# Keys and values by halves of a chunk: narrower scores and outputs in a fused attention and MLP kernel

## The chip, the cores and the metric

The kernel runs on one core of a Trainium2 chip. A core has TensorE (PE in the profile, the matrix engine; PEld is its loading of weights), VectorE (DVE), ScalarE (ACT), GpSimd (POOL) and SyncE (SP, which here only issues DMAs), and 16 DMA engines that SP, ACT and POOL share through queues of their own. The metric is device time in microseconds of one launch. The median of three runs before is 204.6 us (204.56 to 204.68).

## The reference

Two stages follow each other. The first is a linear attention with decay over 4 batches, 8 heads, 768 positions and 64 features, in blocks of 64 positions:

```
Dmask = where(rel >= 0, lam ** rel, 0)            # rel = query position - key position, in a block
intra = (q_block @ k_block.T * Dmask) @ v_block
inter = (q_block * lam ** (pos + 1)) @ kv_state
out   = intra + inter
kv_state = lam ** 64 * kv_state + (k_block * lam ** (63 - pos)).T @ v_block
```

The block size does not change what is computed: a query sees every key at or before its own position, with the weight lam to the power of the distance. The second stage is an MLP over the 3072 rows (4 x 768) of 512 features that come out: `silu(x @ w_in) @ w_out` with 2048 features in between. Inputs and output are float32.

## The kernel before

**The attention.** The kernel works with chunks of 128 positions, and with pairs of chunks: pair n (0 to 11) holds 256 positions of one batch, for all 8 heads. `load_pair` (L426) issues one DMA each for k, q and v of a pair on SP. Partition p of the tile holds positions 2p and 2p + 1 of the pair, for each head, so a row of the transfer is two positions of 64 float32 numbers, 512 bytes. The first chunk is in partitions 0 to 63, the second in 64 to 127 (`halves`), and r = 0 or 1 is the parity of the position.

`prepare` (L526) casts k and q to bfloat16 in `kq` (`cast`, or `cross` from pair 4 on, which swaps heads in the second chunk), scales v by a power of lam in `vd` (`scale_v`, with the constants `lam_v`), and turns kq into `kqT`: by TensorE for pairs 0 to 3 (L578), by a DMA transpose on SP from pair 4 on (L593).

From pair 3 on the matmuls of the attention stand in a `burst` (L603). A burst holds, for the new pair n, the sums of k times v for the state (`state`, L659, named d) and the scores (`score`, L670, named s); and, for the pair before, the outputs from the masked scores (`output`, L626, named o) and from the state (`inter64`, L633, named i). All these matmuls are 64 rows by 64 columns, a quarter of the array, and two lists, `rows[0]` and `rows[1]`, feed the two halves of the array's rows, so that four run at once. A score matmul takes 64 keys of one parity as weights and streams all 128 queries of the chunk, 64 of each parity. An output matmul takes v of 64 keys of one parity as weights and streams the masked scores of these keys, 128 columns. A burst is cut into up to three parts: up to the last output, up to the last score of heads 0 to 3 (k below 2), and the rest. All its banks (two for outputs, one for the state, four for scores) are taken when its first part is placed.

After a part with scores, VectorE multiplies each bank of them with the 0/1 constant `tri` (`mask`, L825, 128x512) into `st`. VectorE evacuates outputs with the powers of lam into `xt`, the input of the MLP (`evac`, L719).

**The MLP.** `product1` (L921) computes x @ w_in, ScalarE applies silu while it empties the banks (L951), and `product2` (L972) computes the second product. For the last 12 units of 128 rows the second product is made by seven products of quarter matrices in place of eight (`product2_of_four`, L1063), for the last 8 units the first product too (`product1_of_four`, L1214). They need sums of quarters of the weights: `sums_of_w_out` (L1035) builds five sums `bsum` of w_out, each in two halves on VectorE or POOL. The same function has a second way, for the sums listed in `BMOVED`: a copy by a DMA on SP and an accumulating DMA issued by POOL. BMOVED is empty here.

**What sets the order.** Everything is a task with a key, a cost per engine, the tasks it depends on and the buffers it needs. `Planner` (L57) replays all tasks by these costs, takes at each engine the ready task with the lowest key, and so writes out one fixed order for each engine and each DMA queue. Two tables correct it by hand or by search: `SHIFT` moves keys, `HOME` pins a task to an engine. Where PE is planned to be idle in the first 19 us, filler matmuls on `ones` are put (L1321).

Of the kernel before, what the change touches and what calls it, by code (L numbers as in the profile page):

```python
# [36 lines left out]
WIDE, CAST, LARGE, PLAIN, TURN = (512, 24.0, 27.0), (256, 14.0, 31.0), (2048, 92.0, 92.0), (2048, 84.0, 84.0), (1024, 46.0, 46.0)  # L37

# [18 lines left out]
class Planner:  # L57
# [8 lines left out]
    SHIFT = {('cast', 10, 1, 0): -0.5, ('cast', 10, 1, 1): -2.5, ('cast', 6): -3.5, ('cast', 7, 1, 0): -1.5, ('first', 2): -0.5,  # L66
             ('first', 2, 6): -8, ('first', 3, 6): -8.5, ('first', 4, 4): 1, ('first', 5, 0): -4, ('first', 5, 6): -0.5,
             ('first', 6): 6.25, ('first', 6, 11): 2.25, ('first', 6, 12): -1, ('first', 6, 14): 13.25, ('first', 6, 15): 2.25,
             ('first', 6, 2): 0.5, ('first', 6, 3): 0.25, ('first', 6, 4): -4.5, ('first', 6, 5): -10.75, ('first', 7): -0.25,
             ('first', 7, 0, 4): 1.75, ('first', 7, 1, 4): 1, ('first', 7, 2, 3): 1, ('first', 8, 0, 5): -4,  # L70
             ('first', 8, 1, 1): -3.5, ('first', 8, 2, 4): 4.5, ('four', 12): 4.5, ('four', 20): -0.75, ('group', 2): 0.25,
             ('group', 3): -5.5, ('group', 7): 4.75, ('group', 8): -7.5, ('load w', 3, 1): -1.5, ('mask', 11): 5.75, ('mask', 5): 3,
             ('mask', 7, 0, 1): 3, ('mask', 8, 0, 0): 5.75, ('mask', 9, 0, 1): 0.25, ('outputs', 0, 0): 4, ('pair', 10): 2.5,
             ('pair', 11): -9.75, ('pair', 4): -7.5, ('pair', 5): -0.75, ('pair', 9): 8.75, ('scale', 3, 0): -1, ('score', 1): 8,
             ('second', 10): 7, ('seven', 12): 0.5, ('seven', 12, 3): -8.25, ('seven', 12, 5): -4.75, ('seven', 16): 3.75,
             ('seven', 20): 3.75, ('silu', 8, 1, 0, 1): 2.75, ('states', 2, 0): 6.75, ('store', 9): -2, ('turn', 3, 0, 1): -10.75,
             ('turned', 1): -7.25, ('u3', 8): 5.5, ('w', 1): 6.75, ('xe', 0, 0, 1): 4.5, ('xe', 11): 11.75, ('xe', 3, 0, 0): 1.5,
             ('xf', 6): -10.25, ('xt', 7, 1): 7, ('y', 10, 0, 0): 5.75}
    HOME = {('a', 16, 1, 1): 'POOL', ('a', 20, 5, 0): 'POOL', ('a', 20, 5, 1): 'POOL', ('b', 3, 1): 'POOL',
            ('cast', 11, 1, 1): 'POOL', ('cast', 3, 0, 1): 'ACT', ('cast', 4, 0, 0): 'DVE', ('cast', 5, 0, 0): 'POOL',  # L80
            ('cast', 5, 1, 0): 'POOL', ('cast', 5, 1, 1): 'ACT', ('cast', 6, 0, 0): 'DVE', ('cast', 6, 1, 0): 'DVE',
            ('cast', 6, 1, 1): 'ACT', ('cast', 7, 1, 0): 'DVE', ('cast', 7, 1, 1): 'ACT', ('cast', 8, 1, 1): 'DVE',
            ('cast', 9, 0, 0): 'POOL', ('cast', 9, 1, 0): 'POOL', ('cast o', 1, 1): 'DVE', ('cast o', 2, 0): 'ACT',
            ('cast o', 2, 1): 'ACT', ('cast w', 1, 3): 'POOL', ('m3', 12): 'DVE', ('result', 1): 'ACT', ('scale', 11, 0): 'POOL',
            ('scale', 9, 0): 'POOL', ('to u', 7, 3): 'DVE', ('turned', 0, 0, 1): 'DVE', ('turned', 0, 1, 0): 'ACT',
            ('u3', 8, 0): 'DVE', ('u3', 8, 1): 'ACT', ('u3', 8, 2): 'ACT', ('w', 3, 0): 'POOL', ('w', 4, 0): 'POOL',
            ('x', 7, 3): 'POOL', ('x', 8, 1): 'POOL', ('xe', 6, 0, 0): 'POOL', ('xe', 6, 0, 1): 'POOL', ('xe', 7, 0, 0): 'ACT',
            ('xf', 10, 0, 1): 'POOL', ('xf', 4, 0, 1): 'DVE', ('xf', 7, 0, 0): 'POOL'}
# [197 lines left out]
def kernel(  # L286
# [10 lines left out]
    nc = tc.nc  # L297
# [12 lines left out]
    AWAY, XAWAY, OWN = range(5,12), (), (0, 1)  # L310
# [5 lines left out]
    BMOVED, POOLED = (), (6,)  # L316
    LOADED, MOVED, HEAD = (4, 9), (12,16), (1.8, 1.8, 1.2, 0.6)
    TKEY, SEVENS, LAG, WSKEY, FIRST_SEVENS = 9.0, 12, 5.0, 14.0, (16,20)
# [77 lines left out]
    lam_be = const.tile([128, NP], F32, name="lam_be")  # L396
    for r in range(2):
        nc.scalar.activation(lam_v[:, :, r], log_all, AF.Exp, scale=pose[:, r:r + 1])
# [27 lines left out]
    def load_pair(key, n, which):  # L426
# [4 lines left out]
        def plain(e, i, g, ms):  # L431
            nc.sync.dma_start(out=tile_of(bufs[i, g], [128, 2 * len(ms), 128], F32, "raw"),
                              in_=src[i][heads(ms)].rearrange("h (p r) d -> p h (r d)", r=2))

        for g, ms in enumerate(parts_of(n)):
            for i in which:
                bufs[i, g] = Buf("rawh" if n in FINE else "raw")
                ts[i, g] = add((key, g, i), {"SP": 0.55}, lambda e, i=i, g=g, ms=ms: plain(e, i, g, ms), bufs=[bufs[i, g]],
                               nbytes=0.131 * len(ms), kind=WIDE,
# [43 lines left out]
    def rates(e):  # L483
        for a in range(NP):
            nc.scalar.activation(lam_xe[:, a, :], row, AF.Exp, scale=log_lam[:, a:a + 1])

# [116 lines left out]
    def burst(n, alone=False):  # L603
# [72 lines left out]
        def queue(row, what, width, fn, *more, part=slice(None)):  # L676
            rows[row].extend([(what, 0.0005 + 0.00044 * width, lambda a=(k, r) + more: fn(*a), k) for k, r in steps][part])
# [708 lines left out]
```

## Time and profile before

| What | Value |
|---|---|
| Median of three runs | 204.6 us (204.56 to 204.68) |
| Profiled execution: its time, its span | 204.5 us, 202.8 us |
| VectorE, ScalarE, POOL busy | 146.2, 123.4, 71.4 us |
| HBM read, written | 27.27 MB, 6.29 MB |
| Packets on SP's DMA queue (q1) | 62400, 34.74 MB, 62.4% of 16 engines' span |
| On ACT's queue (q10), on POOL's (q0) | 7.2%, 14.4% |
| PE matmuls: score L670, output L626, state L659 | 288, 288, 240 |

The span runs from the first to the last instruction; the time has 1.7 us more around it. Busy time of PE counts a matmul from its start to its modelled end, and neighbours overlap. The share of a DMA queue is the sum of its packets' times over 16 engines and the span. A wait is put down to the instruction that ended it.

### The profile page before, as it was taken

How to read it: one execution, taken by the hardware profiler on the slowest of the kernel's cores; microseconds unless marked ns; L12 is line 12 of the kernel's file. 1: busy time of each engine (PE TensorE's matmuls, PEld its weight loads, DVE VectorE, ACT ScalarE, POOL GpSimd, SP SyncE). 2: the span in 40 equal slices, each digit the busy share in tenths (PEclk: the TensorE clock that was granted, in tenths of full speed). 3: DMA queues.
4: the chain of work that ended last, by engine and by line, in shares of the span. 5: the costliest groups of instructions: out<-in, count | busy, mean ns of one | idle time of the engine just before them, and what ended most of it. 6: DMA issues, size and time to landing. Idle time of an engine off the chain costs nothing.

```text
span 202.8 us, 6082 instructions
## 1 busy us (share of the span) xinstructions
PE 196.8 (97%) x2585; PEld 145.3 (72%) x2585; DVE 146.2 (72%) x231; ACT 123.4 (61%) x193; POOL 71.4 (35%) x84
## 2 busy tenths in 40 slices
PE   6999999999999999999999999999999999999993
PEld 2776887867865557557776465458888888888882
DVE  3697749778994949599795875969765766743972
ACT  3697887849785655705384626683796878564010
POOL 4105430222560400058766041338954372000800
PEclk9999999999999999999999999999999999999999
DMA  4999999999999999899999471119997967111324
GB/s 110 339 335 366 386 362 334 368 313 382 230 282 261 318 344 298 208 311 218 303 255 213 130 128 33 57 58 222 176 184 184 218 179 136 52 55 52 107 103 155
DMA packets 71658, 44.43 MB, mean 219 GB/s; under 512 B 18448, under 2 KB 64528, under 8 KB 71632
## 3 DMA queue, kind: packets, MB, share of 16 engines
q1 hardware_dynamic: 62400, 34.74, 62.4%
q0 software_dynamic: 5456, 4.46, 14.4%
q10 hardware_dynamic: 3776, 4.86, 7.2%
q8 instruction: 20, 0.33, 0.6%
q14 instruction: 6, 0.05, 0.1%
HBM read 27.27 MB, written 6.29 MB: 165 GB/s over the span
## 4 chain that ended last, share of the span: by engine, by line
PE 90%; DVE 5%; issue 2%; ACT 1%; ACTq 0%
PE banks L935 27%; PE banks L1126 18%; PE banks L977 17%; PE banks L1254 12%; PE banks L1321 4%; PE banks L626 2%; PE banks L670 2%; PE banks L578 2%; DVE kq L409 1%; DVE xt L414 1%; PE banks L633 1%; DVE st L414 1%; PE banks L659 1%; PE banks L848 1%; PE banks L898 1%
## 5 line engine op out<-in xcount | busy, mean ns | idle before, releaser
L935 PE MATMUL banks<-xt,w_in_bf 128*128 128x256 bf16 (+1 forms) x448 | 67.4, 288 | 0.4 <-DVE xt L414 0.2
L951 ACT ACTIVATE g<-banks 128x512 bf16<-128x512 f32 x64 | 46.0, 745 | 26.8 <-PE banks L935 25.4
L935 PEld LDWEIGHTS <-w_in_bf 128*128 128x128 bf16 x448 | 42.9, 98 | 15.3 <-issue 0.8
L977 PE MATMUL banks<-w_out_bf,g 128*128 128x512 bf16 x192 | 49.6, 379 | 0.0
L414 DVE TENSOR_TENSOR st<-banks,tri 128x512 bf16<-128x512 f32 (+1 forms) x42 | 29.9, 757 | 3.7 <-PE banks L670 2.9
L977 PEld LDWEIGHTS <-g 128*128 128x128 bf16 x192 | 18.3, 98 | 19.1
L414 DVE TENSOR_TENSOR xt<-banks,lam_xe 128x512 bf16<-128x512 f32 x24 | 16.0, 684 | 12.5 <-PE banks L626 12.3
L1126 PE MATMUL banks<-bsum,g 128*128 128x256 bf16 x160 | 21.2, 273 | 0.0
L407 ACT ACTIVATE kq<-raw 64x512 bf16<-64x512 f32 (+3 forms) x24 | 18.5, 799 | 2.7 <-DMA raw<-in_k_dram 1.2
L407 ACT ACTIVATE osb<-banks 128x512 f32<-128x512 f32 (+1 forms) x15 | 8.7, 582 | 17.5 <-PE banks L977 12.2
L1126 PEld LDWEIGHTS <-asum 128*128 128x128 bf16 x176 | 17.2, 98 | 2.0
L409 DVE CAST kq<-raw 64x512 bf16<-64x512 f32 (+3 forms) x21 | 15.2, 741 | 4.0 <-DMA raw<-in_k_dram 2.5
L1126 PEld LDWEIGHTS <-g 128*128 128x128 bf16 x160 | 15.6, 98 | 1.9
L414 POOL TENSOR_TENSOR xf<-y,lam_be 128x256 f32<-128x256 f32 (+1 forms) x11 | 8.2, 749 | 22.1 <-DVE y L789 21.9
L1017 DVE TENSOR_TENSOR asum<-g 128x1024 bf16<-128x1024 bf16 x11 | 9.1, 836 | 8.3 <-PE banks L1126 2.9
L1270 ACT ACTIVATE g<-tmp 128x512 bf16<-128x512 f32 x16 | 12.4, 774 | 3.5 <-DVE tmp L1017 3.3
L1017 DVE TENSOR_TENSOR tmp<-banks,tmp 128x512 f32<-128x512 f32 x16 | 11.0, 687 | 4.8 <-PE banks L1254 4.1
L414 DVE TENSOR_TENSOR vd<-raw,lam_v 128x1024 bf16<-128x1024 f32 (+1 forms) x11 | 12.3, 1120 | 3.0 <-DMA raw<-in_v_dram 2.9
L1254 PE MATMUL banks<-xsum,wsum 128*128 128x256 bf16 x96 | 14.4, 273 | 0.0
L1017 POOL TENSOR_TENSOR asum<-g 128x1024 bf16<-128x1024 bf16 x3 | 6.4, 2121 | 22.8 <-PE banks L1126 19.1
L1254 PEld LDWEIGHTS <-wsum 128*128 128x128 bf16 x128 | 12.4, 98 | 1.5
L1321 PE MATMUL banks<-ones 128*128 128x128 bf16 (+1 forms) x85 | 11.0, 277 | 1.9 <-DVE ones L358 1.5
(96 smaller groups left out, 294.6 us busy)
## 6 DMA issues: line engine op xcount, KB each, us to landing
raw<-in_k_dram SPq DMA_DIRECT2D x11, 512.0 KB, 5.4
raw<-in_q_dram SPq DMA_DIRECT2D x11, 512.0 KB, 6.1
raw<-in_v_dram SPq DMA_DIRECT2D x11, 512.0 KB, 7.6
out_dram<-osb ACTq DMA_DIRECT2D x18, 256.0 KB, 3.6
raw_w<-in_moe_w_in_dram SPq DMA_DIRECT2D x8, 512.0 KB, 8.0
raw_w<-in_moe_w_out_dram SPq DMA_DIRECT2D x8, 512.0 KB, 6.6
asum<-g SPq DMA_DIRECT2D x8, 256.0 KB, 2.6
asum<-g POOLq DMA_DIRECT2D x8, 256.0 KB, 5.1
```

The source lines that it names most:

```text
L407: nc.scalar.activation(o, i, AF.Copy)
L409: nc.vector.tensor_copy(o, i)
L414: (nc.vector if e == "DVE" else nc.gpsimd).tensor_tensor(o, a, b, op=AL.mult)
L578: nc.tensor.transpose(t[:, r, m, :], kq_of()[:, i, r, 2 * m:2 * m + 2, :], ident)
L935: nc.tensor.matmul(t[:, j, :], lhsT=w_in_bf[:, ko, 128 * m:128 * m + 128], rhs=xt[gi].tile[:, ko, :], start=(ko == 0), stop=(ko == KI - 1))
L951: nc.scalar.activation(t.rearrange("p j (c a r) -> p (j c) r a", c=n // U, r=2), psum_of(bank).rearrange("p (jc r a) -> p jc r a", r=2, a= ...
L977: nc.tensor.matmul(psum_of(bank), lhsT=gs[gi, ko][1](1, 128 * gp, 128)[:, 0], rhs=w_out_bf[:, ko], start=(ko == 0), stop=(ko == KO - 1))
L1017: (nc.vector if e == "DVE" else nc.gpsimd).tensor_tensor(o, x, y, op=op)
L1126: nc.tensor.matmul(part(bank, u), lhsT=lhs(u), rhs=b_of(ko), stop=ko == 7, skip_group_check=True, start=opens and not ko and not u)
L1254: nc.tensor.matmul(two_of(bank)[:, f], lhsT=(wb[0].tile if wb else w_quarter(*wl))[:, ko, fs], rhs=(xsum(xr) if isinstance(xr, int) else x ...
L1270: nc.scalar.activation(t.rearrange("p j (c a r) -> p (j c) r a", c=2, r=2), src().rearrange("p (jc r a) -> p jc r a", r=2, a=64), AF.Silu)
L1321: nc.tensor.matmul((t if b.pool == "bank" else t[:, 0])[:, 0:w], lhsT=ones[:, 0:128], rhs=ones[:, 0:w], start=True, stop=True)
```

## The change

In pairs 4 to 11 (`SPLIT`) k and v are laid out by halves of a chunk in place of parities: a partition holds, for each chunk, one position of its first half and one of its second. q keeps its layout. Rows of the k and v transfers are one position, 256 bytes, and each transfer is three DMAs: one of 128 partitions for the two middle quarters of the pair, and two of 64 partitions for the first and the last quarter. In the first chunk the early half is at r = 0, in the second at r = 1, so the code takes `r ^ i` or `r ^ c` where it means early (0) or late (1).

No query of a chunk's first half can see a late key. So the scores of late keys are made for late queries alone (64 columns in place of 128), in a layout of their own: banks of group 0 hold the early keys of all heads, banks of group 1 the late keys, and the masked scores `st` and the outputs follow this. The masks of group 1 are 128x256. New constants `lam_s` and `tri_s` serve the new order of positions. The two banks of group 1 are taken only when the part of the burst that first writes them is placed. The order inside a burst has the early keys of all heads ahead of the late ones.

BMOVED becomes (1, 7, 6), so three of the five sums of w_out are made by DMAs. The tables SHIFT and HOME are replaced as a whole, so the planner's order differs from beginning to end: pairs 5, 7 to 11 stand later among the matmuls, pairs 4 and 6 a little earlier.

```diff
+HALF = (256, 16.5, 16.5)
...
-    SHIFT = {...}
-    HOME = {...}
+    SHIFT = {...}
+    HOME = {...}
...
+    SPLIT = range(4, 12)
...
-    BMOVED, POOLED = (), (6,)
+    BMOVED, POOLED = (1, 7, 6), (6,)
...
         def plain(e, i, g, ms):
+            if n in SPLIT and i != 1:
+
+                t = tile_of(bufs[i, g], [128, 2 * len(ms), 128], F32, "raw")
+                x = src[i][heads(ms)].rearrange("h (s a) d -> a s h d", a=64)
+                nc.sync.dma_start(out=t[:, :, 64:128], in_=src[i][heads(ms), 64:192].rearrange("h p d -> p h d"))
+                for c, p in enumerate(halves):
+                    nc.sync.dma_start(out=t[p, :, 0:64], in_=x[:, 3 * c])
+                return
             nc.sync.dma_start(out=tile_of(bufs[i, g], [128, 2 * len(ms), 128], F32, "raw"),
                               in_=src[i][heads(ms)].rearrange("h (p r) d -> p h (r d)", r=2))
...
+    def split_rates(e):
+        for r in range(2):
+            nc.scalar.activation(lam_s[:, :, r], log_all, AF.Exp, scale=pose_s[:, r:r + 1])
+
+    def split_masks(e):
+        for c, r in enumerate(halves):
+            nc.gpsimd.iota(spot_s[r], pattern=[[64 - 128 * c, 2]], base=64 * c, channel_multiplier=1)
+        nc.gpsimd.tensor_scalar(pose_s, spot_s, -1.0, 64.0, op0=AL.mult, op1=AL.add)
+        nc.gpsimd.memset(tri_s, 1.0)
+        for r in halves:
+            nc.gpsimd.affine_select(
+                out=tri_s[r], in_=tri_s[r], compare_op=AL.is_ge, fill=0.0,
+                base=0, pattern=[[1, 2], [2, 64]], channel_multiplier=-1,
+            )
...
-                 lam_v[:, hs, :, None].to_broadcast([128, n_h, 2, 64]))
+                 (lam_s if n in SPLIT else lam_v)[:, hs, :, None].to_broadcast([128, n_h, 2, 64]))
...
                 for h, d in enumerate(halves):
-                    nc.tensor.matmul(psum_of(ob[c])[d, U * k:U * k + U], lhsT=o["vd"].tile[halves[c], 2 * k + h, r, :],
-                                     rhs=o["st"][k // 2].tile[halves[c], 2 * h + k % 2, U * r:U * r + U],
+                    to = psum_of(ob[c])[d, U * k:U * k + U]
+                    if o["n"] not in SPLIT:
+                        by = o["st"][k // 2].tile[halves[c], 2 * h + k % 2, U * r:U * r + U]
+                    else:
+                        by = o["st"][r].tile[halves[c], 4 * h + k]
+                        if r:
+                            to = to.rearrange("d (q i) -> d q i", q=2)[:, :, 32:]
+                    nc.tensor.matmul(to, lhsT=o["vd"].tile[halves[c], 2 * k + h, r ^ c if o["n"] in SPLIT else r, :], rhs=by,
                                      start=first_in(boxes[c], h), stop=True, skip_group_check=True)
...
-            db, sb_ = Buf("bank", n % NB != NB - 1), [[Buf("bank", True) for _ in halves] for _ in range(2)]
+            db, sb_ = Buf("bank", n % NB != NB - 1), [[Buf("bank", not g or n not in SPLIT) for _ in halves] for g in range(2)]
...
-            bufs += [db, kq, vd, kqT] + sum(sb_, [])
+            bufs += [db, kq, vd, kqT] + (sb_[0] if n in SPLIT else sum(sb_, []))
+            late_bufs = sb_[1] if n in SPLIT else []
...
                     h = row ^ i if n in CROSSED else row
+                    if n in SPLIT:
+
+                        t = psum_of(sb_[r][h])[:, 0:4 * U // (1 + r)].rearrange("p (m q i) -> p m q i", m=4, q=2)
+                        nc.tensor.matmul(t[c, k], lhsT=t_of()[halves[row], 0, r ^ i, k, c],
+                                         rhs=t_of()[halves[row], 1, :, k, c.start + 32 * r:c.stop], start=k == 0, stop=True,
+                                         skip_group_check=True)
+                        continue
...
+                if new and late_bufs and any(what == "s" and k for what, k, _, _ in order[prev:cut]):
+                    bufs, late_bufs = bufs + late_bufs, []
...
+                        if n in SPLIT:
+                            t = tile_of(st, [128, 8, U // (1 + g)], BF16, "st")[:, 4 * h:4 * h + 4]
+                            mult(e, t.rearrange("p m (q i) -> p m q i", q=2),
+                                 psum_of(b)[:, 0:4 * U // (1 + g)].rearrange("p (m q i) -> p m q i", m=4, q=2),
+                                 tri_s[:, :, 0:64 // (1 + g)][:, None].to_broadcast([128, 4, 2, 64 // (1 + g)]))
+                            return
...
+    masks_s = add((-4.9, 0), {"POOL": 1.2}, split_masks, tag="masks s")
...
+    rates_s = add((-3.2, 0), {"ACT": 0.4}, split_rates, deps=[masks_s], tag="rates s")
```

## The prediction

> **What bounds the kernel now.** I read the page from the top: busy shares, slices, chain.
>
> ```profile
> span 202.8 us, 6082 instructions
> PE 196.8 (97%) x2585; PEld 145.3 (72%) x2585; DVE 146.2 (72%) x231; ACT 123.4 (61%) x193; POOL 71.4 (35%) x84
> ...
> PEclk9999999999999999999999999999999999999999
> DMA  4999999999999999899999471119997967111324
> ...
> PE 90%; DVE 5%; issue 2%; ACT 1%; ACTq 0%
> ```
>
> TensorE (PE) is busy 97% of the span at the full granted clock and is 90% of the chain that ended last. A busy PE need not be a PE at its peak, so I asked next what PE waited for; this is the whole answer.
>
> ```profile
> PE banks L1321 <- DVE ones L358: 1.5, 1, 1.5
> PE banks L1321 <- DVE st L414: 0.3, 1, 0.3
> PE banks L935 <- DVE xt L414: 0.2, 1, 0.2
> PE banks L898 <- PE banks L879: 0.2, 1, 0.2
> PE banks L626 <- PE banks L633: 0.2, 1, 0.2
> ```
>
> Behind the first 31 us there is hardly a wait. The end is set by the length of PE's instruction stream, and PE time saved there is a gain of the same size, as long as nothing new makes PE wait. The other resource at its limit is the DMA; these rows of the table by stretches give span, PE, PEld, DVE, ACT, POOL, clock, DMA share (over 1 where queues overlap) and GB/s.
>
> ```profile
> 31.00:62.00 31.00, 31.00 (x384) 23.15 (x377) 25.91 (x38) 24.29 (x38) 9.87 (x10) 1.00 1.08 319
> 62.00:112.00 50.00, 49.67 (x733) 31.80 (x731) 38.84 (x60) 25.80 (x40) 19.68 (x21) 1.00 1.12 269
> 112.00:143.00 31.00, 31.00 (x461) 18.68 (x459) 24.31 (x42) 18.01 (x28) 11.82 (x14) 1.00 0.50 108
> ```
>
> Until 112 us the 16 DMA engines are full, then half idle. PE does not notice, since its order takes every pair well behind the pair's arrival. So two sums are wanted: PE's work, and how much later the loads may come.
>
> **Scores and outputs (L670, L626).** The change makes the matmuls of late keys 64 columns wide in place of 128, in pairs 4 to 11. Their matmuls use a quarter of the array each, four at a time. The price of a width is in the timeline of before, where some of L761 are 64 wide and L898 and L626 are 128 wide (start, duration, ..., count):
>
> ```profile
> 10.02 0.32 PE L761 MATMUL banks<-vd,kq 64*64 64x64 bf16 x16
> 15.99 0.44 PE L761 MATMUL banks<-vd,kq 64*64 64x64 bf16 x32
> 20.23 0.42 PE L898 MATMUL banks<-st,vd 64*64 64x128 bf16 x16
> 108.05 0.64 PE L626 MATMUL banks<-st,vd 64*64 64x128 bf16 x32
> ```
>
> 16 more matmuls are four quartets: (0.44 - 0.32)/4 = 30 ns for a quartet 64 wide, (0.64 - 0.42)/4 = 55 ns for one 128 wide. A pair has 32 score and 32 output matmuls, that is 8 quartets of each, and half of them become short: 8 x 25 ns = 0.2 us a pair, 1.6 us over eight pairs. All of it lies on the path. Both ends of this price: nothing, if the strided 2x32 writes into the bank cost what the narrower stream saves (no row shows such a write); 8 x 8 x 27.5 = 1.8 us if a short one takes exactly half. I take 1.6, since both rows are of this array form.
>
> **Banks taken later.** Only the last part of a burst now asks for the two banks of the second half. In the order of the changed kernel's instructions PE has 29 visits to quartet work where it had 27 (pair 3's burst and pair 7's are cut in two, with other matmuls between). A visit costs filling and draining: the visit of before from 107.54 to 109.14 in the chain is 1.60 us with 112 matmuls (28 quartets; the 24 state matmuls beside scores cost less than full ones, so the two rows of the array add up to 0.22 + 1.14 = 1.36), which leaves 0.24. Two more: 0.5 us lost. Two more filler matmuls (L1321) are 0.1.
>
> **Masks (L414 on st).** The 16 masks of late keys shrink from 128x512 to 128x256: 757 ns by their group against 359 to 399 ns for other 128x256 VectorE results, so about 0.36 x 16 = 5.8 us less on VectorE. Three sums of w_out (six of the ten bsum instructions, L1017: 1081 ns on VectorE, 2549 on POOL) become DMAs, of which VectorE is spared five: 5.4 us more. VectorE is 72% busy and not on the path, so I count nothing for it directly, but the only late stall of PE, between 90.5 and 92.0 (about 0.65 us longer than the matmuls need), is for xt behind two slow casts on VectorE. The whole order is laid out anew, so that place is gone and another may appear: between 0 and 0.65 us of gain I take 0.3.
>
> **New constants.** Six small POOL instructions (two iota, one tensor_scalar, one memset, two selects; their like in before took 0.31 + 0.28 + 0.31 + 0.89 = 1.8 us) go where POOL is idle from 3.2 to 9.5 us. Two Exp on ScalarE (0.49 us for the two of L398) go into its idle 0.84 us ahead of the first kqT copy at 6.44. Cost nothing; without that cover 0.5 us, since the kqT copy leads to the first scores.
>
> **Loads.** A load of k or v becomes three DMAs: 16 loads, 32 more issues on SP at 0.45 to 0.57 us, some 16 us of SP, which is not the limit: one pair is 7 issues (3.5 us) and one transpose (2.7 to 4.8 us) per 10 us of transfers. The row size falls from 512 to 256 bytes, 1024 packets to 2048. In the packet records of before, SP's queue took (medians) 27 ns for 512 bytes, 46 for 1024 and 84 for 2048: 8 ns and 37 ns per KB, so 17.5 ns for 256. The 16,384 packets of 256 bytes there (the transposes of kq) have a median of 18 and a mean of 28. Bounds: 17.5 and 28. I take 18, because loads lie on the straight line of the loads and a transpose is another kind of transfer. Then a split load takes 2048 x 18/16 = 2.3 us for 1.75, and 16 of them add 9 us to a full queue.
>
> Does PE feel it? Adding transfers in SP's order (512 KB loads 1.75, weights 1.34, transposes 3.6 us from 2.8 us on) puts the end of the transposes of pairs 4 to 10 in before at 57.6, 68.2, 77.0, 87.7, 94.8, 103.6 and 112; the trace has their packets at 52-57, 60-68, 72-76, 84-88, 88-96, 100-104 and 112-116, so the sum holds within some 2 us. For the changed order the same sum gives 57.5, 73.8, 79.1, 91.4, 103.6, 111.3, 119.0 and 128.4 for pairs 4 to 11. PE's bursts move too: counting the matmuls ahead of each (109 ns for 256 columns, 216 ns for 512), they stand 0.3 earlier, 4.8 later, 2.0 earlier, then 3.1, 3.1, 2.6, 0.9 and 4.9 later, so near 62.2, 78.8, 85.0, 99.6, 110.3, 118.8, 125.8 and 140.1. With 1 us to land, the margins are 3.7, 4.0, 4.9, 7.2, 5.7, 6.5, 5.8 and 10.7 us, where late pairs had over 11 before. Hidden, but with half of the cover gone. Pair 10 has 15 split loads ahead of its transpose, so 5.8 us are used up at 5.8/15 = 0.39 us more per load: 3 ns more per packet, 21 ns. That is the point from which the loads decide.
>
> The three sums by DMA (three copies on SP, three accumulates on POOL, 512 KB each) come behind the last v load, when the share has fallen to 0.5. The asum copies queue behind them on SP; in before they wait for activations until 134.7, so 2 x 1.75 us ahead costs nothing. The transpose of pair 11 shares the engines with two accumulates: 1024 packets of 65 ns (POOL's queue) are 4.2 us each, within its 10.7.
>
> [...]
>
> **Sum.** -1.6 (columns) + 0.5 (visits) + 0.1 (fillers) - 0.3 (stall) = -1.3 us. The profiled execution took 204.5 us (span 202.8 and 1.7 around it), 0.1 under the median of 204.6. So 203.2 on the profiled one, 203.3 for the median.
>
> **The rivals.**
> 1. The gain is eaten (no change, 204.2 to 205.0): the visits stay, the head of 31 us, where PE follows VectorE and ScalarE, loses 0.5 to 1 us by its new order. For it: the first 31 us have the PE waits of before. Against: POOL and ScalarE have gaps there that the new instructions fit. About 204.6.
> 2. The loads come late (slower): 256-byte packets cost over 21 ns. At 28 ns, (28 - 21) x 2048/16 x 15 = 13.4 us: 217. At 24.5 ns half of that: 210. For it: the full DMA until 112 us and the mean of 28. Against: the line through three sizes and the median of 18.
> 3. The late banks make PE wait (slower). The last part of eight bursts asks for two banks while the matmuls behind it on PE, of any kind, stand in line; if a bank still waits for its eviction (745 ns for a silu, 684 for xt) PE stands for half of one, 0.35 us, each time: 8 x 0.35 = 2.8 us against 1.3, so 206.1. It decides from 1.3/8 = 0.16 us a burst. For it: four score banks were all taken ahead of the burst before, so this wait could not occur there. Against: PE's idle time after 31 us was 0.65 us in all, so evictions as a rule come in time.
>
> **How the numbers follow.** Forecast 0.58 (own range 202.4 to 204.0), no change 0.12, late loads 0.12, late banks or other waits of that size 0.18. A median of this kernel can be told from another from about 0.2% (0.4 us). Faster is the first, same the second, slower the sum of the last two, 0.30. Low: 1.8 + 0.65 us gained and one visit fewer gives 202.3. High: late banks at 0.4 us each give 206.6; beyond it lie most of the late loads (0.10), some of the late banks (0.04) and 0.06 lie under the low end.
>
> **What would show it.** Right: PE's share stays at 97% or above, short score and output quartets at 30 ns, PE's waits after 31 us under 1 us in sum, 256-byte load packets at 18 ns, the DMA row full until about 120 us. Wrong: PE waiting for kq, vd or kqT (late loads), PE's quartets waiting inside a burst for ACT or DVE on banks (late banks), 256-byte packets over 21 ns, or short quartets at 55 ns.

## The result and the profile after

The changed kernel takes 223.22 us (median of 6 runs, 222.31 to 225.27) against 204.58 us for the kernel before (6 runs, 204.49 to 204.68): a ratio of 1.092, interval 1.087 to 1.097. It is 18.6 us slower, where 1.3 us of gain was forecast, and far outside the range. The profiled execution took 225.27 us, 2.05 over the median. Ratios leave out executions that took over 1.5% more than the fastest of the same kernel (two of eight in e4, two of ten in f3, two of four in g4, one each in e7 and h2), so some differ a little from the quotient of the medians beside them, which take in all. In the changed kernel the same operations have other line numbers: L991 and L1033 are the plain matmuls of the two products, L1310 and L1182 those of the groups of units that are made by seven products of quarter matrices (Winograd groups below), L708 the scores in the layout by halves, L662 the outputs, L1382 the fillers.

The head of the page, after:

```profile
span 223.6 us, 6126 instructions
PE 199.9 (89%) x2574; PEld 145.4 (65%) x2587; DVE 139.1 (62%) x234; ACT 121.4 (54%) x190; POOL 69.7 (31%) x89
...
PEclk9999999999999999999999999999969967999999
DMA  4999999999999999999799999999999789702244
...
PE 44%; DMA 30%; SPq 14%; DVE 4%; POOL 3%; issue 2%; ACT 1%; POOLq 0%; DVEq 0%
```

TensorE falls from 97 to 89% of the span, and the chain that ended last is now 30% DMA and 14% SP's queue, neither of which was in it before. The DMA row is full until about 173 us, where it had been half idle from 112 to 143. The granted clock drops in three slices late in the span. The answer on what PE waited for (us in total, times, longest) gives the places:

```profile
PE banks L1182 <- DMA asum<-g: 8.2, 2, 5.6
PE banks L708 <- DMA kqT<-kq: 4.4, 2, 3.5
PE banks L1382 <- DVE ones L359: 1.5, 1, 1.5
PE banks L1033 <- POOL w_out_bf L417: 1.1, 1, 1.1
PE banks L991 <- POOL w_in_bf L417: 1.0, 1, 1.0
```

g is the output of silu, which the second product reads. For two of its three Winograd groups (units 12 to 19) the sums of quarters of g, `asum`, are made by the DMA: copies on SP and accumulating DMAs issued by POOL. The first line is the wait for these sums, the second is late loads of k and q (kqT is the transposed pair). Both had no line before. Around the first wait the table by stretches (columns as in the prediction) shows the other loss:

```profile
160.00:180.00 20.00, 14.13 (x114) 11.41 (x112) 9.37 (x14) 9.22 (x15) 8.47 (x10) 0.91 1.03 160
180.00:200.00 20.00, 17.28 (x138) 14.63 (x139) 7.36 (x12) 10.64 (x17) 7.57 (x7) 0.83 0.74 132
```

PE is not only idle there but slow, at a granted clock of 0.91 and 0.83, and the busy time itself is longer: its matmuls of 256 columns take 213 ns from start to start where this trace has the clock at a half, 109 elsewhere. The two waits are 12.6 us, and the lower clock over these 40 us is worth by estimate up to 1.8 + 3.4 us more (20 x 0.09 and 20 x 0.17).

The packet records of the trace say what became of the transfers. On SP's queue the mean of a 512-byte packet is 28.0 ns before and 32.2 after; of the 256-byte packets of the loads by halves the median is 18 to 19 ns, about the forecast, but the mean is 22 to 23 in the stretches of 8 us that hold no transpose (40 to 48 and 64 to 72 us). What makes the reading turn is when this begins: already in the first 40 us, where no load by halves exists and the loads are those of before, 512-byte packets have a mean of 30.5 to 32.7 ns in stretches of 8 us, for 27.0 to 28.2 before. Something makes packets longer that the diff does not touch.

### The profile page after: what moved, and what is told of

It reads as the page before. It is cut to its first block, busy times and chain, and to the rows that moved or that the text cites. A ratio compares the mean times of both kernels' runs of the same rounds, so it can differ in the third digit from the quotient of the medians.

```text
span 223.6 us, 6126 instructions
## 1 busy us (share of the span) xinstructions
PE 199.9 (89%) x2574; PEld 145.4 (65%) x2587; DVE 139.1 (62%) x234; ACT 121.4 (54%) x190; POOL 69.7 (31%) x89
## 4 chain that ended last, share of the span: by engine, by line
PE 44%; DMA 30%; SPq 14%; DVE 4%; POOL 3%; issue 2%; ACT 1%; POOLq 0%; DVEq 0%
PE banks L1182 14%; PE banks L991 12%; PE banks L1033 11%; DMA asum<-g 10%; DMA raw_w<-in_moe_w_out_dram 6%; DMA bsum<-w_out_bf 5%; SPq L622 5%; PE banks L1310 4%; SPq L446 4%; DMA raw_w<-in_moe_w_in_dram 3%; DMA kqT<-kq 3%; DMA raw<-in_q_dram 2%; SPq L1106 2%; SPq L444 2%; DVE st L420 2%
## 5 line engine op out<-in xcount | busy, mean ns | idle before, releaser
L991 PE MATMUL banks<-xt,w_in_bf 128*128 128x256 bf16 (+1 forms) x447 | 60.9, 288 | 1.1 <-POOL w_in_bf L417 1.0
L1007 ACT ACTIVATE g<-banks 128x512 bf16<-128x512 f32 x64 | 45.6, 742 | 15.9 <-PE banks L991 11.7
L991 PEld LDWEIGHTS <-w_in_bf 128*128 128x128 bf16 x448 | 42.8, 98 | 15.4 <-issue 1.2
L1033 PE MATMUL banks<-w_out_bf,g 128*128 128x512 bf16 x180 | 42.7, 379 | 2.2 <-POOL w_out_bf L417 1.1
L1033 PEld LDWEIGHTS <-g 128*128 128x128 bf16 x192 | 18.0, 98 | 19.4 <-issue 0.2
L413 ACT ACTIVATE kq<-raw 64x512 bf16<-64x512 f32 (+2 forms) x24 | 18.5, 799 | 21.0 <-DMA raw<-in_q_dram 12.3
L1182 PEld LDWEIGHTS <-asum 128*128 128x128 bf16 x176 | 18.1, 104 | 11.7 <-DMA asum<-g 8.8
L1182 PE MATMUL banks<-bsum,g 128*128 128x256 bf16 x160 | 23.0, 275 | 0.4 <-DMA g<-g 0.4
L1182 PE MATMUL banks<-w_out_bf,asum 128*128 128x256 bf16 x96 | 14.7, 305 | 8.2 <-DMA asum<-g 8.2
L420 DVE TENSOR_TENSOR st<-banks,tri_s 128x512 bf16<-128x512 f32 (+1 forms) x32 | 15.9, 547 | 6.1 <-ACT kq L413 6.0
L417 POOL CAST kq<-raw 64x512 bf16<-64x512 f32 (+1 forms) x14 | 10.6, 778 | 28.3 <-DMA raw<-in_k_dram 16.0
L415 DVE CAST kq<-raw 64x1024 bf16<-64x1024 f32 (+3 forms) x20 | 13.5, 686 | 9.0 <-DMA raw<-in_k_dram 5.0
L1169 POOL DMA_DIRECT2D asum<-g x8 | 13.6, 1843 | 16.6 <-DMA asum<-g 11.5
L1182 PEld LDWEIGHTS <-g 128*128 128x128 bf16 x160 | 15.5, 99 | 2.6 <-DMA g<-g 0.6
L1326 ACT ACTIVATE g<-banks 128x512 bf16<-128x512 f32 x16 | 11.6, 740 | 7.6 <-PE banks L1310 7.6
L1310 PE MATMUL banks<-xsum,wsum 128*128 128x256 bf16 x96 | 15.0, 285 | 0.5 <-POOL xsum L1073 0.4
L1310 PEld LDWEIGHTS <-wsum 128*128 128x128 bf16 x128 | 13.0, 102 | 3.2 <-issue 0.5
L1169 POOL DMA_DIRECT2D g<-g x8 | 14.8, 2577 | 0.0
L413 ACT ACTIVATE tmp<-banks 128x512 f32<-128x512 f32 x11 | 6.6, 596 | 14.3 <-PE banks L1310 13.7
```

Source lines behind the costliest of these rows:

```text
L413: nc.scalar.activation(o, i, AF.Copy)
L415: nc.vector.tensor_copy(o, i)
L420: (nc.vector if e == "DVE" else nc.gpsimd).tensor_tensor(o, a, b, op=AL.mult)
L991: nc.tensor.matmul(t[:, j, :], lhsT=w_in_bf[:, ko, 128 * m:128 * m + 128], rhs=xt[gi].tile[:, ko, :], start=(ko == 0), stop=(ko == KI - 1))
L1007: nc.scalar.activation(t.rearrange("p j (c a r) -> p (j c) r a", c=n // U, r=2), psum_of(bank).rearrange("p (jc r a) -> p jc r a", r=2, a= ...
L1033: nc.tensor.matmul(psum_of(bank), lhsT=gs[gi, ko][1](1, 128 * gp, 128)[:, 0], rhs=w_out_bf[:, ko], start=(ko == 0), stop=(ko == KO - 1))
```

## The experiments

**What the four new constants move.** In the programs as built, the addresses of the tiles in a partition of SBUF (bytes) are

```
                  w_in_bf   = n x 256      first raw tile
before             28160      110          a multiple of 256
after              28800      112.5        128 past a multiple of 256
```

spot_s, pose_s, lam_s and tri_s take 32 + 32 + 64 + 512 = 640 bytes ahead of w_in_bf, two and a half times 256. Every tile allocated behind them, the buffers of the loads, of g and of the sums included, sits 128 bytes past a multiple of 256. In the kernel before, an unused tile `pad` of 384 bytes ended the constants on such a multiple. Shrinking it by 128 bytes in the changed kernel puts all these tiles back on multiples of 256; the instructions of every engine stand in the same order. (The older constants between `pad` and the new ones move by 128 bytes with it. They lie off the multiples in the kernel before as well, and no transfer touches them.)

Run e1_after_aligned:

```diff
-    const.tile([128, 96], F32, name="pad")
+    const.tile([128, 64], F32, name="pad")
```

> The kernel after with one number changed: the unused constant tile pad is 64 float32 in place of 96, so that the 640 bytes of new constants move every later tile by 512 bytes and not by 640, back to a multiple of 256. Orders of all engines are the same as in the kernel after. Theory 'addresses' (the new constants put all tiles 128 bytes past a multiple of 256, and DMA rows into them cost more): 512-byte packets of SP's queue fall from a mean of 31 to 27 ns already in the first 40 us, and the time falls from 223 to my forecast, 202.3 to 205. Rival 'loads' (256-byte rows are slow in themselves, pairs come late): 220 to 225 as before the edit, packets unchanged. A time halfway, 210 to 215, would say that both have a share.

Measured: 209.29 us (207.77 to 209.89), ratio to the kernel before 1.021 [1.017, 1.025]. So 13.9 of the 18.6 us hang on the addresses. Its page:

```profile
span 207.6 us, 6139 instructions
PE 196.8 (95%) x2587; PEld 144.2 (69%) x2587; DVE 135.2 (65%) x234; ACT 121.2 (58%) x190; POOL 72.6 (35%) x89
...
PE 84%; DMA 9%; SPq 4%; issue 1%; POOL 0%; ACT 0%; POOLq 0%
```

and what PE waited for:

```profile
PE banks L1182 <- DMA asum<-g: 3.3, 1, 3.3
PE banks L1382 <- DVE ones L359: 1.5, 1, 1.5
PE banks L991 <- POOL w_in_bf L417: 1.4, 1, 1.4
```

No wait for kqT is left, and the one for the sums of g is 3.3 us where it was 8.2. The 512-byte packets are back at a mean of 28.4 ns, and the 256-byte load packets have a median and, in stretches without a transpose, a mean of 18, as forecast.

The other way round, the kernel before with its tiles shifted (e2 by 128 bytes, e3 by 64; nothing else differs):

```diff
-    const.tile([128, 96], F32, name="pad")
+    const.tile([128, 128], F32, name="pad")     # e2
+    const.tile([128, 112], F32, name="pad")     # e3
```

> The kernel before with pad of 128 float32 in place of 96: every later tile lies 128 bytes past a multiple of 256, nothing else differs. Theory 'addresses': 512-byte packets go from 27 to about 31 ns in the mean and the time rises, by less than in the kernel after, since the loads of late pairs have over 10 us of margin and no three sums of w_out go by DMA: 206 to 216. Rival 'loads': 204.6, no change.

> The kernel before with pad of 112 float32: later tiles lie 64 bytes past a multiple of 256. Theory 'addresses' with a boundary of 256 bytes: slow like e2 (206 to 216), since a 512-byte row then touches three blocks of 256 as well. If the boundary that matters is 64 bytes: 204.6. Rival 'loads': 204.6.

Measured: e2 207.34 us, ratio 1.013 [1.010, 1.016]; e3 207.76 us, ratio 1.015 [1.013, 1.017]. A tile that nobody uses makes the tuned kernel 2.7 to 3.1 us slower. 64 bytes past the multiple are as bad as 128 (207.76 and 207.34 us). In e2 the mean 512-byte packet of SP's queue is 31.3 ns for 28.0, in e3 31.4, so the smaller shift is not the cheaper one and the growth is 12% at both; the 256-byte packets of the loads have a mean of 22 to 23 ns in the changed kernel for 18 in e1. By its time e3 is slow like e2, as its expectation gave for a boundary of 256 bytes; for one of 64 it gave 204.6 us. How the address makes a packet longer is not shown by any run.

Why then 13.9 us in one kernel and 2.7 in the other? Two runs divide it. f2 keeps the shifted addresses and takes the 256-byte rows away:

```diff
-            if n in SPLIT and i != 1:
+            if False:
```

> The changed kernel as it stands (tiles 128 bytes past a multiple of 256), with k and v of the late pairs loaded by one DMA of 512-byte rows each; the rows land in another order than the tables of constants expect, so the output is not the reference's; the order of instructions is the same. It tells whether the 14 us that the addresses cost come through the loads by halves or through all transfers. If through the 256-byte rows alone (their records at this address 21 to 38 ns in the mean for 18), the cost of the address falls to what it is in the kernel before (2.8 us) and the time to 209 to 211.5 us. If through all transfers, the copies and accumulates of the sums above all: the wait for kqT (4.4 us) goes, the wait for the sums of g (8.2 us) stays at 5 or more, and the time is 215 to 219 us.

Measured: 212.28 us (211.71 to 212.58), ratio 1.035 [1.031, 1.039], between the two expectations: the wait for kqT is gone, that for the sums is 4.4 us.

```profile
PE banks L1182 <- DMA asum<-g: 4.4, 1, 4.4
PE banks L1382 <- DVE ones L359: 1.5, 1, 1.5
```

Its twin with aligned addresses is e5 below (207.23), so the shift costs 5.0 us with 512-byte rows, 13.9 with the loads by halves. h3 keeps the shifted addresses and the halves and leaves out all sums by DMA (the edits of e4 and f1 below, on the changed kernel):

> The changed kernel as it stands (tiles 128 bytes past a multiple of 256), with the DMAs of both kinds of sums left out as in the aligned run without them (203.8 us); nothing else is changed. It tells what the addresses cost where no sum needs the queue. If they work through the sums alone: 204 to 206.5 us. If they make the loads late by themselves: a wait for kqT of 2 us or more is left and the time is 207 to 212 us.

Measured: 210.38 us (209.44 to 211.34), ratio 1.026 [1.022, 1.029]. Its aligned twin h2 below takes 203.78, so the addresses cost 6.6 us without any sum in the queue:

```profile
PE banks L708 <- DMA kqT<-kq: 3.2, 1, 3.2
PE banks L1382 <- DVE ones L359: 1.5, 1, 1.5
PE banks L1033 <- POOL w_out_bf L417: 1.1, 1, 1.1
PE banks L991 <- POOL w_in_bf L417: 1.0, 1, 1.0
```

The loads are late by themselves (3.2 us for kqT, and casts of the first weights), and with the sums behind them the lateness is paid once more, at the sums of g. The price of the same shift grows as the cover shrinks: 2.7 us in the kernel before, 5.0 with the new order and long rows, 6.6 with short rows and no sums, 13.9 with both.

**The other 4.7 us.** The aligned kernel is at 209.3, not at the 203.3 of the forecast. In its trace 5.2 us more than the matmuls need are lost between 160 and 180 us. The chain of waits of e1 there (start, duration, what):

```profile
151.40 3.51 PE banks L1182 x32
...
154.92 6.66 DMA asum<-g
...
162.15 5.21 DMA asum<-g
...
167.41 0.83 PE banks L1182 x6
168.24 0.68 PE banks L1310 x4
168.92 0.85 PE banks L1182 x4
169.77 2.32 PE banks L1310 x12
```

A 256 KB copy of SP's takes 6.66 us and the accumulate of POOL's queue that follows 5.21, and PE waits for it until 167.4. From 168.1 to 171.3 us the matmuls of 256 columns then take some 210 ns from start to start, not 109. In the kernel before the same chain begins earlier; these rows are the accumulates in the answer on the tile asum (min, median and max in ns of POOL's issue, first and last start), of before

```profile
L1113 POOL DMA_DIRECT2D asum<-g x8: 848/1308/2873, 137.9 to 166.8; - x8
```

and of e1:

```profile
L1169 POOL DMA_DIRECT2D asum<-g x8: 859/2037/4296, 143.9 to 174.2; - x8
```

Two suspects stand in the queue: the three new sums of w_out by DMA (e4) and the longer time of the loads by halves (e5). Each run takes one away from e1, in the same order of instructions.

```diff
-                    nc.sync.dma_start(out=tile_of(b, [128, 8, 256], BF16, "bsum"), in_=b_quarter(*qs[0]))
+                    pass
...
-                    nc.gpsimd.dma_start(out=b.tile, in_=b_quarter(*qs[1]), accum_op=AL.add)
+                    pass
```

> e1 (aligned) without the six DMAs of the three w_out sums: the copies on SP and the accumulates on POOL are left out, and the products that use these sums take the first quarter of w_out alone in their place (that part of the output is another). The order of everything else on all engines is that of e1. In e1 PE waits 3.3 us for an asum accumulate at 163.8 us and then runs at a lower clock. Theory 'sums by DMA' (the three accumulates hold POOL's queue, so that the asum accumulates behind them land late): the wait goes and the time falls to 203.5 to 204.5. Rival 'order' (the asum chain of activation, SP copy and POOL accumulate is too short of time in this order whatever stands ahead): still a wait of 2 to 4 us, 207.5 to 209.5.

```diff
-            if n in SPLIT and i != 1:
+            if False:
```

> e1 (aligned) with the loads of before: k and v of pairs 4 to 11 as one DMA each with 512-byte rows (so k and v lie in the wrong order and the attention of these pairs is another one). Orders of PE, VectorE, ScalarE and POOL are those of e1. Theory 'addresses' with rows that are hidden once they are aligned (18 ns a packet, no wait for kqT in e1): within 1 us of e1, 208 to 210. Rival 'rows': 2 us or more below e1.

Measured: e4 206.82 us (205.88 to 209.2), ratio 1.008 [1.005, 1.011]; e5 207.23 us (206.14 to 208.24), ratio 1.011 [1.008, 1.015]. Each gives back 2.1 to 2.5 us of the 4.7, and in both the wait for the sums shrinks from 3.3 to 2.0 us without going away. The queue that e5 unburdens is seen in the pages, where the first rows of the DMA queues (packets, MB, share of 16 engines) are, in e1,

```profile
q1 hardware_dynamic: 82688, 36.58, 70.1%
```

and in e5:

```profile
q1 hardware_dynamic: 65792, 36.57, 63.6%
```

70.1% of 207.6 us are 145.5, 63.6% of 205.5 us are 130.7: the same bytes take 14.8 us more of the queue's time by halves. At 18 ns the load packets alone are 37 us for 28, the 9 us of the forecast; the rest is in packets that run beside them (the mean of the weights' 2048 bytes, for one, is 94.7 ns in e1 and 90.2 in e5).

e7 makes the sums of w_out on VectorE and GpSimd again, as before, with the order planned anew:

```diff
-    BMOVED, POOLED = (1, 7, 6), (6,)
+    BMOVED, POOLED = (), (6,)
```

> e1 (aligned) with BMOVED empty as in the kernel before, so that all five sums of w_out are built by VectorE and POOL; the planner lays out the order anew with the same tables. It computes everything. Theory 'sums by DMA': no long wait for asum, 203 to 205.5, with VectorE 6 us busier. Rival 'order': the wait stays, 207 to 210.

Measured: 208.01 us (207.01 to 211.82), ratio 1.014 [1.010, 1.018]. The sums by DMA are not the whole of it: 2.3 us of wait for the sums of g stay. So f1 takes that chain itself away from e1 (no copies, no accumulates, the matmuls read x; these are 24 transfers, 8 copies and 16 accumulates, of the first two of the three Winograd groups), and h2 both kinds of sums (f1 and e4 together):

```diff
-      ... nc.sync.dma_start(out=t(), in_=x(4)),
+      ... None,
...
-                            nc.gpsimd.dma_start(out=x(4) if here else t(), in_=y(4), accum_op=AL.add)
+                            pass
```

> The changed kernel with its addresses put back to multiples of 256 bytes, with the sums of g of the last two Winograd groups (twenty copies and accumulates by DMA, asum) left out: the matmuls read one of the two summands, so the product is not the reference's; the order of everything else is the same. Theory: what the aligned kernel (209.3 us) still lost beside the forecast of 203.3 is the late end of this chain, a 3.3 us wait and the slow matmuls behind it, 5.2 us in the stretch from 160 to 175 us. Then 203.0 to 204.5 us, with no wait of TensorE over 1.5 us after 100 us. Rival: TensorE waits for the next thing instead (outputs, evictions, the sums of w_out), and the time stays over 206.5.

> The changed kernel at addresses that are multiples of 256 bytes, with the DMAs of both kinds of sums left out (six of w_out, twenty of g; the matmuls read one of the two summands, so the product is not the reference's), in the same order. If the forecast's terms for the matmuls, the banks and the loads were right and only these sums hold the kernel back: 202.8 to 203.8 us, without the 1.0 us wait for kqT that remained when only the sums of g were left out. If the halves cost more than was forecast: 204.2 us or more, as without the sums of g alone.

Measured: f1 204.51 us (203.31 to 206.17), ratio 0.999 [0.996, 1.001]; h2 203.78 us (203.18 to 208.28), ratio 0.996 [0.994, 0.997]. All that PE waits for in h2:

```profile
PE banks L1382 <- DVE ones L359: 1.5, 1, 1.5
PE banks L991 <- POOL w_in_bf L417: 0.6, 1, 0.6
PE banks L811 <- DVE vd L420: 0.2, 1, 0.2
PE banks L662 <- PE banks L668: 0.2, 1, 0.2
```

Without both kinds of sums (h2) the changed kernel is on the faster side, within 0.5 us of the forecast. In f1 a wait of 1.0 us for kqT is left (pair 10), in h2 none. Both do less work than the others, so they show where the time is and are no kernels to use. The kernel before has no wait for its sums of g, and this one loses 4.8 us at them (209.3 less 204.5): that is the distance of 4.7 us from the kernel before. The four runs give the price of each sum twice. The sums of w_out by DMA cost 2.5 us (209.3 less 206.8) where sums of g stand behind them and 0.7 (204.5 less 203.8) where not, which is not clear of the noise, since the intervals of f1 and h2 overlap; the sums of g cost 4.8 with the others ahead and 3.0 without.

Whether the sums of g of the second of the two groups (units 16 to 19) would be better off the DMA was tried with everything computed, e1 with

```diff
-    ... MOVED, HEAD = (4, 9), (12, 16), ...
+    ... MOVED, HEAD = (4, 9), (12,), ...
```

(f3; f4 also with BMOVED empty), planned anew:

> Addresses put back to multiples of 256 bytes, and the sums of g of the last Winograd group made by VectorE and GpSimd in place of DMA copies and accumulates (those of the group before it stay with the DMA); the order is planned anew, and everything is computed. Theory (the chain of DMA sums of the last group is what ends late): 203.5 to 206.5 us, without the 3.3 us wait for asum after 160 us; VectorE and GpSimd gain some 4 to 7 us of work each. Rival (the whole order behind the sums is short of time, whoever adds): 207 to 210 us, with the wait now on VectorE or GpSimd.

> As the run with the last group's sums of g on VectorE and GpSimd, and the three sums of w_out on these engines too, no longer by DMA; planned anew, everything computed. If the DMA queues' load in 120 to 160 us is what makes the chain late, this is the fastest of the aligned ones: 203 to 205.5 us. If VectorE and GpSimd run short of time with both, 206 to 210 us, with waits on them.

Measured: f3 206.93 us (205.30 to 211.13), ratio 1.008 [1.005, 1.012]; f4 208.13 us (207.42 to 209.14), ratio 1.016 [1.010, 1.021]. In f3 the wait for asum is gone from the list of PE's waits, and between 160 and 170 us PE is busy all 10.00 us at clock 1.00:

```profile
160.00:170.00 10.00, 10.00 (x94) 8.97 (x92) 6.69 (x11) 8.56 (x15) 2.12 (x1) 1.00 0.44 89
```

Its profiled execution took 205.55 us, within what the theory gave (203.5 to 206.5); the median of all ten lies 0.4 above. f4 has less load on the DMA yet is not faster, with short waits on ScalarE and VectorE in its place (0.6, 0.6 and 0.5 us). f3 is the fastest variant of the change that computes everything, and it is still slower than the kernel before.

Last, the order itself. SHIFT and HOME, the lists that move single instructions in the plan, were replaced with the change. g1 puts the lists of before (and its sums of w_out) on the halves at aligned addresses; g4 puts the new lists and the sums by DMA on the kernel before:

```diff
-    SHIFT = {('a', 16, 7, 0): 2, ('a copy', 12, 2, 1): -7.75, ('a copy', 16, 2, 0): -12, ('cast', 6, 1, 0): -1,
+    SHIFT = {('cast', 10, 1, 0): -0.5, ('cast', 10, 1, 1): -2.5, ('cast', 6): -3.5, ('cast', 7, 1, 0): -1.5, ('first', 2): -0.5,
...
```

> The halves of k and v (loads, masks, narrow matmuls, banks taken later) and the new constants, at addresses that are multiples of 256 bytes, but with the lists of shifts and homes of the kernel before and its sums of w_out on VectorE and GpSimd; planned anew, everything computed. Theory (the new lists, with the sums by DMA, bring the sums of g of the last groups late, and the halves themselves do what the forecast said): 203.0 to 205.0 us, without a wait of TensorE for asum over 1 us. Rival (the halves themselves, by the queue's time, push the chain back in any order): 207 us or more, with a wait for asum of 2 us or more.

> The kernel before with the changed kernel's lists of shifts and homes and its three sums of w_out by DMA, without the halves and without the new constants (addresses as before). Theory (the order and the sums by DMA make the loss that the addresses leave): 207 to 210 us, with a wait for asum of 2 to 4 us after 155 us and slow matmuls behind it. Rival (the halves make it): 204 to 205.5 us.

Measured: g1 213.54 us (212.73 to 213.79), ratio 1.043 [1.040, 1.045]; g4 211.31 us (207.52 to 214.30), ratio 1.019 [1.013, 1.026]. The ratio of g4 rests on two executions, of 207.52 and 209.77 us. Both kernels are slower than the one before, and this pair does not tell the two causes apart: a list made for one kernel spoils the other. In g1 PE waits most in the Winograd groups of the first product (lines are one off here, so L1311 is L1310):

```profile
PE banks L1311 <- ACT tmp L414: 2.2, 4, 1.0
PE banks L1183 <- DMA asum<-g: 1.6, 2, 1.2
PE banks L1383 <- DVE ones L360: 1.5, 1, 1.5
PE banks L1311 <- DVE banks L416: 1.4, 1, 1.4
```

That is more than the wait for asum. In g4 the time of the two executions is the one that the theory gave (207 to 210), but in its trace, that of the execution of 214.3 us, PE waits 1.9 us for kqT and never for asum. So neither expectation is met by its own reason. One thing the traces do tell: the start of the first accumulate of g goes with the lists. It is 137.9 us in the kernel before and 137.0 in g1, with the old lists, and 143.0 to 145.8 in e1, e4, e5, e7 and g4, with the new ones, with and without the halves and the sums of w_out by DMA. Open stays what the late start alone costs, and how much of the loss would come with the halves in an order that is written for them.

**The matmuls alone.** e6 is e4 with late keys 128 columns wide again in scores and outputs, in the same banks and order:

```diff
-                        t = psum_of(sb_[r][h])[:, 0:4 * U // (1 + r)].rearrange("p (m q i) -> p m q i", m=4, q=2)
+                        t = psum_of(sb_[r][h])[:, 0:4 * U].rearrange("p (m q i) -> p m q i", m=4, q=2)
...
-                                         rhs=t_of()[halves[row], 1, :, k, c.start + 32 * r:c.stop], start=k == 0, stop=True,
+                                         rhs=t_of()[halves[row], 1, :, k, c], start=k == 0, stop=True,
```

> e4 with the late keys' matmuls 128 columns wide again: scores for all queries, outputs over all columns from the early keys' masked scores (another output), masks unchanged in size, orders as in e4. It prices the narrowing alone. By the rows of the kernel before (30 ns for a quartet 64 wide, 55 for 128) it is 1.6 us slower than e4, if PE is the bound in both. If narrow matmuls gain nothing: equal to e4 within 0.3 us.

Measured: 208.11 us (206.88 to 209.15), ratio 1.016 [1.012, 1.019], against 1.008 [1.005, 1.011] for e4: 1.3 us for the narrow columns by the medians, 1.6 by the ratios, whose intervals all but touch, where 1.6 was expected. Part of it may be masked: the later PE waits less for the sums of g (0.7 us, and 1.0 for a neighbouring accumulate, for 2.0 in e4), and e6's trace has no stretch at half clock there, where e4's has one of 3.4 us.

## Why the prediction was wrong, by its own steps

- **Scores and outputs (-1.6): right.** The timeline of h2 has short scores at the price taken from before (start, duration, count at the end; the row is of scores):

```profile
87.01 0.32 PE L708 MATMUL banks<-kqT 64*64 64x64 bf16 x16
```

  Summed over the matmuls at their own lengths (109 ns for 256 columns, 216 for 512, a quarter of the width for the quartets), PE's stream is 182.97 us before and 181.38 in h2: 1.59 less. That is a count by widths, not a measurement; e6 measures 1.3 to 1.6. The strided writes cost nothing that shows in the row above.
- **Banks taken later (+0.5): right in kind, small in size.** What quartets lose beyond their own length is 8.03 us before and 8.89 in h2, so 0.9 for 0.5. Columns, banks and the two new fillers together are 0.7 us less PE time where 1.0 was forecast. No wait of a score for an eviction appears in e1 or h2, so the third rival did not happen.
- **Masks (-0.3): of the right size, but no run isolates it.** Between 80 and 100 us PE lost 0.86 us beyond its plain matmuls before, 0.58 in h2 and 0.19 in e1, with other work in these 20 us; in h2 no wait for xt is left.
- **New constants ("cost nothing"): the step that failed.** They were priced by their eight instructions on POOL and ScalarE and the cover of these. What they cost is their 640 bytes: 13.9 us (209.3 to 223.2), through the start addresses of all tiles behind them. The prediction never asked where the later tiles come to lie, although an unused tile `pad` among the constants was there to be asked about.
- **Loads (18 ns a packet, hidden): right on aligned addresses, with less cover than forecast, and wrong in the kernel as it stands.** In e1 the load packets are 18 ns, and no pair is late; but the transpose of pair 10 landed at 125.0 us for a burst at 127.0, a margin of 2.0 where 5.8 was forecast, and in f1 it is 1.0 us late. In the changed kernel their mean, 22 to 23 ns, passes the 21 that the prediction named as the point of decision, and the wait for kqT appears, 4.4 us. The second rival (late loads, 210 to 217) has the right place, but for another reason than the size of the packets: shifted 512-byte rows grow as well (28.0 to 31.3 ns in e2). In e1 the medians are 18 ns for a packet of 256 bytes and 27 for one of 512.
- **Three sums by DMA ("cost nothing"): wrong.** They cost 2.5 us. The estimate looked at the engines' share (0.5 from 112 us on in the kernel before) and at SP's queue at 134.7, but took the stretch as it was before. These sums fill the stretch themselves: the DMA share at 120 to 140 us is 0.37 before, 0.54 in e4, with the halves but without the sums, and 1.19 in e1. So their copies and accumulates and the last transpose run into the sums of g. The nine extra us of queue, called hidden, are hidden from the pairs and not from these: e5 gives 2.1 us for them.
- **The sum.** In h2, which leaves out all sums by DMA, the rest of what the forecast listed comes to 203.8 us for 203.3. The miss of 19.9 us is the addresses (13.9), the two kinds of sums by DMA (5.5, from 203.8 to 209.3; the chain of the sums of g was treated as unchanged) and these 0.5. No rival had the addresses; that the second one, late loads, has the right place is luck.

## What to carry to other kernels

A new tile can cost more than the instructions that fill it, since whatever is allocated behind it moves: 640 bytes of constants cost 13.9 us here. So compare the start addresses of DMA buffers before and after; in this case 512-byte packets of SP's queue took a mean of 28.0 to 28.4 ns into tiles on multiples of 256 bytes, and 30.9 to 32.4 at 64 or 128 bytes past one. A transfer that is hidden from its own reader can still take time from the next user of the same queue (the sums of w_out, for which PE had no wait in e1, cost 2.5 us with the sums of g behind them), so follow the queue to its last user, not to the one that was changed. And before the parts of a slow change are judged, look at a transfer that the change did not touch: here the 512-byte packets of the first 40 us, 30.5 to 32.7 ns for 27.0 to 28.2, told that the cause was not local.

## What the runs showed of the hardware

- The time of a packet changed with the start address in SBUF: 512 bytes on SP's queue took a mean of 28.0 ns in the kernel before and 28.4 in e1, at multiples of 256 bytes, 30.9 to 32.4 at 128 past (f2, e2, the changed kernel, h3) and 31.4 at 64 past (e3). 512-byte packets of POOL's accumulates went from 65 to 71 ns (e1 to the changed kernel).
- A pause of PE cost more than its length. In e4, after a wait of 2.0 us, the matmuls of 256 columns ran at some 215 ns from start to start for 3.5 us, but for the first six (start, duration, count, and the wait in brackets):

```profile
162.88 0.38 PE L1310 MATMUL banks<-xt,w_in_bf 128*128 128x256 bf16 x2
165.28 0.86 PE L1182 MATMUL banks<-w_out_bf,asum 128*128 128x256 bf16 x6 [2.02 <-DMA asum<-g]
165.95 1.05 PE L1310 MATMUL banks<-xsum,wsum 128*128 128x256 bf16 x4
...
169.44 0.60 PE L1310 MATMUL banks<-xsum,wsum 128*128 128x256 bf16 x4
```

  Four take 1.05 us where 0.60 is usual; between 160 and 180 us PE loses 3.9 us in all, 2.0 of them waiting. The granted clock (last column but two; the others as in the prediction) shows it in stretches of 3.41 us, in e4

```profile
162.53:165.94 3.41, 1.39 (x13) 1.00 (x12) 1.30 (x2) 1.81 (x3) 3.41 (x3) 1.00 1.34 217
165.94:169.36 3.42, 3.42 (x18) 2.15 (x16) 0.69 (x1) 0.47 (x1) 1.75 (x3) 0.50 0.91 165
```

  and in e7, where a wait of 2.3 us (165.5 to 167.8) left it at 1.00:

```profile
162.88:166.29 3.41, 2.58 (x24) 2.06 (x22) 2.29 (x4) 3.17 (x6) 3.41 (x4) 1.00 0.81 139
166.29:169.71 3.42, 1.48 (x12) 1.09 (x12) 0.70 (x2) 0.49 (x1) 2.43 (x4) 1.00 1.08 172
```

  Within the spans of these runs' traces the clock is halved for 3.41 us at a time (once for two such stretches), and the starts lie on one grid of 3.41 us in each trace. Over this grid the next stretch was at half clock behind each of the nine with 2.0 us or more without a matmul, behind none with 1.83 us or less, and behind two of the three between (1.87 to 1.93). The wait of e7 is divided between two stretches, and so is the longest wait for kqT in the changed kernel (3.5 us, from 114.0), which left the clock at 1.00 too. So in these traces it mattered where on the grid a pause fell. Of the four executions of e1 two have a mean granted clock of 0.992 and two of 0.999 or more; that their pauses fell differently on the grid is not shown, since only one of them has a trace.
